# First-layer blocks 5 to 8 as two block pairs by seven products, instead of 7 and 8 alone

## The chip, the cores and the metric

One core of a Trainium2 chip. The metric is the device time of one execution in microseconds, as the median of several runs; the runs of the kernel before lie between 1590.37 and 1594.31 us. PE is TensorE (PEld its weight loads), DVE VectorE, ACT ScalarE, POOL GpSimd, SP SyncE, whose queue issues the DMAs.

## What is computed

Linear attention followed by two feed-forward layers, cut here to what matters:

```
kv  = einsum('bhsd,bhse->bhde', k, v)                 # B=8, H=8, S=576, D=64
o   = einsum('bhsd,bhde->bhse', q, kv)
x   = o / sqrt(mean(o*o, -1) + 1e-6) * g_norm         # then as 4608 tokens x 512
h   = x @ w_in1;   y   = (s * relu(h)**2 + b) @ w_out1    # 512 -> 2048 -> 512
h2  = y @ w_in2;   out = (h2 * sigmoid(h2)) @ w_out2      # 512 -> 2048 -> 512
```

The weights come as 8-byte floats and are turned into float32 by integer operations in the kernel. A product of float32 precision is made of three matmuls: every operand is split into a rounded part (hi) and a remainder (lo), and hi\*hi + hi\*lo + lo\*hi is accumulated.

## The kernel before

**Tiling.** The 4608 tokens are NB = 9 blocks of T = 512 tokens, features on the partitions. Block 8 collects the last 64 tokens of each of the 8 batches. A layer on one block alone ("plain") is 16 units of 128 hidden features (`unit`, L697 to L790): per unit 4 x 3 matmuls make h in a PSUM bank, ACT applies relu, square, scale and bias in place (L730, L733, L736) and rounds (L217), DVE makes the remainder `gh` (L220), and 4 x 3 matmuls add to the four output banks `acc`. That is 24 matmuls of 128 x 512 per unit, 384 per block.

**Pairs.** Two blocks go through a layer together by seven products instead of eight (Strassen-Winograd, a 2 x 2 product of token blocks by feature halves). The names are those of the code. Weights: eight factors A11, A12, A21, A22, S1 to S4 per set; a set covers one kind (in or out), one layer and two of the 16 weight tiles, so there are 32 sets (`factors`, L361 to L418). It recovers or decodes the four quarters, makes four sums (L393), rounds (L217) and makes remainders (L220), and stores all to DRAM in `w_d`. Tokens: B11, B21, B22 and T1 to T4, the last four from four subtractions (`pair_sums`, L846 to L873, over DRAM `xt_d`); `pair_x` loads them, rounds on ACT and makes the remainder on DVE or POOL.

Within a pair there are 8 steps j. `hidden(tp, j)` (L920 to L1028) does 7 x 2 x 3 matmuls into three PSUM banks X, Y, Z (line 936, `hp`), which hold sums of products; DVE adds them up (L961) into SBUF tiles `tmp`, ACT applies the function, differences T1 to T4 are made from `tmp` tiles on DVE or POOL (L1000), and each of seven g matrices is rounded on ACT (L217) and its remainder made on DVE or POOL (L220). `outputs(tp, q)` (L1049 to L1083) takes two steps j together: 14 groups of 6 matmuls, each into an `acc` bank which DVE adds to a running sum (L1073). `results` (L1085 on) adds up the seven sums on POOL (L1098) and stores them; for a first-layer pair it also makes the four token differences for the second layer in place (L1115). A pair is 8 x 42 + 4 x 84 = 672 matmuls.

**Order before.** First layer: blocks 0 to 6 plain, then blocks (7, 8) as a pair. Second layer: pairs (0,1), (2,3), (4,5), (7,8), then block 6 plain. NL1 (L174) is the number of first-layer pairs; `base(tp)` is the key at which pair tp begins, 112 + 32 tp.

**Beside the plain blocks** run: attention in 32 pairs of heads (`attention_pair`, eight batches by four), of which block t's are due during block t - 1; the decoding of the first layer's weights (`decode`); all 32 factor sets, spread evenly from key 19 to key 92; and the normalizing of block 8 (`last_block`). One unit is one key.

**What sets the order.** The program is written out by hand through `Plan` (L20 on): each operation has engines it may run on with a cost, a key, what it needs and makes, and the buffers that it takes and gives. `run` goes through them in simulated time, always takes the earliest that can begin (of those within 0.02 us the smallest key), and so fixes one order for every engine and for the SP queue. On the chip each engine works through its list in that order and waits by semaphores. A cost marked `Port` may not overlap another such cost in the plan; `both` lets DVE or POOL do it, `both2` also, without that mark.

**Buffers.** PSUM has eight banks: `acc` 4, `h` 2, `at` 2; in a pair X and Z come from `h`, Y from `at`. In SBUF 9 `tmp` tiles, 8 `rq` and 4 `rh` tiles of 128 x 256 for factors. Tiles of the first layer's resident weights are lent to the pairs when no plain block needs them any more (`lent_to`).

```
    NTMP = 9
    NRQ, NRH = 8, 4
...
    BANK = (X, Y, Z, X, Y, Y, Z)
...
        read = {3: "x1", 4: "u2", 5: "u3", 6: "h22"}
```

The last line says which product may only start when a DVE or ACT operation has read the bank that it adds to.

## Time and profile before

| what | value |
|---|---|
| runs shown, median of 3 | 1591.52 us |
| profiled execution: time / span of its instructions | 1591.99 / 1590.2 us |
| busy, of the span: PE, DVE, ACT, POOL | 99%, 67%, 57%, 44% |
| matmuls | 7500 |
| moved by DMA | 351 MB, 221 GB/s on average |

The span runs from the first to the last instruction of the program. A busy share is an average over stages of different kind. The PE figure counts a matmul from its start to its modelled end, and matmuls overlap, so the distance between starts tells what one costs. PEclk in the windows is the TensorE clock that was granted: 1.00 is 2.4 GHz, 0.50 is 1.2 GHz.

### The profile page before, as it was taken

The numbers are of one execution on the slowest core, as the hardware profiler recorded it, in microseconds if no ns is written. First come the engines' busy times: TensorE is split into PE (matmuls) and PEld (weight loads), VectorE is DVE, ScalarE is ACT, GpSimd is POOL, SyncE is SP. The second block draws the span as 40 slices with busy tenths as digits, with TensorE's granted clock in tenths as the row PEclk, the third lists the DMA queues.
The fourth block names the chain that finished last, engine by engine and source line by source line (L and its number), as shares of the span: only waits on it lengthen the run. The fifth ranks groups of instructions, "written<-read, shape, count | busy, mean of one in ns | idle before, by whom it ended". The sixth has DMA issues, their size and how long they took to land.

```text
span 1590.2 us, 23417 instructions
## 1 busy us (share of the span) xinstructions
PE 1572.8 (99%) x7500; PEld 1282.3 (81%) x7500; DVE 1068.8 (67%) x1811; ACT 898.5 (57%) x1720; POOL 693.5 (44%) x560
## 2 busy tenths in 40 slices
PE   8999999999999999999999999999999999999999
PEld 6877887878888888887888788888888888888887
DVE  5887677767767876535668966885688568856521
ACT  5997666666666777556767443545354445444222
POOL 1332121111122221123567886786678658865510
PEclk9999999999999999999999999999999999999999
DMA  8765767777677885896668786878687868876684
GB/s 214 196 190 155 249 209 239 225 207 220 197 202 226 247 235 169 287 350 213 189 194 260 230 271 194 284 200 236 188 295 194 238 194 261 199 240 188 210 210 134
DMA packets 377147, 351.31 MB, mean 221 GB/s; under 512 B 178240, under 2 KB 288832, under 8 KB 377024
## 3 DMA queue, kind: packets, MB, share of 16 engines
q1 hardware_dynamic: 376896, 349.81, 73.8%
q8 instruction: 60, 0.98, 0.3%
q14 instruction: 63, 0.52, 0.1%
q0 software_dynamic: 128, 0.00, 0.0%
HBM read 254.28 MB, written 95.42 MB: 220 GB/s over the span
## 4 chain that ended last, share of the span: by engine, by line
PE 88%; DMA 6%; DVE 2%; SPq 2%; ACT 2%; issue 1%; POOL 0%; DVEq 0%; ACTq 0%; POOLq 0%
PE hp L936 23%; PE acc L1064 8%; PE acc L1066 8%; PE acc L1065 8%; PE h L212 6%; PE h L213 6%; PE h L214 6%; PE acc L212 6%; PE acc L213 5%; PE acc L214 5%; SPq L229 2%; PE kv_ps L496 1%; PE acc L769 1%; PE acc L767 1%; PE acc L768 1%; DMA tmp<-y 1%
## 5 line engine op out<-in xcount | busy, mean ns | idle before, releaser
L936 PE MATMUL hp<-xo,win 128*128 128x512 f32 x1680 | 424.0, 390 | 2.9 <-DVE tmp L961 2.9
L936 PEld LDWEIGHTS hp<-xo,win 128*128 128x128 f32 x1680 | 315.1, 188 | 72.3 <-DVE tmp L961 4.6
L220 POOL TENSOR_TENSOR g<-tmp,g 128x512 fp32r<-128x512 f32 x168 | 238.2, 1426 | 223.6 <-ACT g L217 219.4
L1073 DVE TENSOR_TENSOR ya<-acc,ya 128x512 f32<-128x512 f32 x210 | 142.9, 685 | 116.7 <-PE acc L1066 116.2
L1064 PE MATMUL acc<-g,wout 128*128 128x512 f32 x560 | 219.6, 392 | 0.1
L1066 PE MATMUL acc<-g,wout 128*128 128x512 f32 x560 | 218.9, 391 | 0.0
L1065 PE MATMUL acc<-g,wout 128*128 128x512 f32 x560 | 218.9, 391 | 0.0
L217 ACT ACTIVATE g<-tmp 128x512 fp32r<-128x512 f32 x280 | 172.6, 629 | 78.4 <-POOL tmp L1000 31.2
L730 ACT ACTIVATE h<-h 128x512 f32<-128x512 f32 x128 | 74.6, 583 | 215.2 <-PE h L214 214.7
L212 PE MATMUL acc<-gh,wo 128*128 128x512 f32 x448 | 182.4, 407 | 0.7 <-DVE y L226 0.5
L212 PE MATMUL h<-xh,wi 128*128 128x512 f32 x448 | 176.9, 395 | 0.0
L213 PE MATMUL acc<-gh,wo 128*128 128x512 f32 x448 | 175.5, 392 | 1.2 <-DVE gh L220 1.2
L213 PE MATMUL h<-xl,wi 128*128 128x512 f32 x448 | 175.8, 392 | 0.2 <-DVE xl L220 0.2
L214 PE MATMUL h<-xh,wi 128*128 128x512 f32 x448 | 175.7, 392 | 0.0
L214 PE MATMUL acc<-gh,wo 128*128 128x512 f32 x448 | 175.0, 391 | 0.0
L961 DVE TENSOR_TENSOR tmp<-hp,tmp 128x512 f32<-128x512 f32 x200 | 136.6, 685 | 52.6 <-PE hp L936 49.2
L220 DVE TENSOR_TENSOR g<-tmp,g 128x512 fp32r<-128x512 f32 x112 | 150.7, 1365 | 18.3 <-ACT g L217 17.4
L322 POOL TENSOR_TENSOR rq<-raw 128x256 uint32<-128x256 uint32 x72 | 46.9, 652 | 253.3 <-DVE raw L308 133.5
L1000 POOL TENSOR_TENSOR tmp<-tmp 128x512 f32<-128x512 f32 x86 | 135.5, 1583 | 29.3 <-ACT tmp L982 15.5
L982 ACT ACTIVATE tmp<-tmp 128x512 f32<-128x512 f32 x120 | 75.5, 629 | 125.6 <-DVE tmp L961 125.2
L1066 PEld LDWEIGHTS acc<-g,wout 128*128 128x128 f32 x560 | 105.2, 188 | 23.4
L1064 PEld LDWEIGHTS acc<-g,wout 128*128 128x128 f32 x560 | 105.1, 188 | 23.3 <-DVE ya L1073 0.8
(137 smaller groups left out, 2682.0 us busy)
## 6 DMA issues: line engine op xcount, KB each, us to landing
wout<-wo SPq DMA_DIRECT2D x312, 256.0 KB, 3.7
win<-wi SPq DMA_DIRECT2D x120, 512.0 KB, 4.7
wi<-rq SPq DMA_DIRECT2D x192, 128.0 KB, 2.3
wo<-rq SPq DMA_DIRECT2D x192, 128.0 KB, 2.5
win<-wi SPq DMA_DIRECT2D x72, 256.0 KB, 3.7
raw<-in_moe_w_out_dram SPq DMA_DIRECT2D x38, 256.0 KB, 3.5
raw<-in_moe_w_in_dram SPq DMA_DIRECT2D x34, 256.0 KB, 3.5
xt_d<-tmp SPq DMA_DIRECT2D x32, 256.0 KB, 5.5
```

The costliest lines, as they stand in the source:

```text
L212: nc.tensor.matmul(ps, wh, xh, start=first, stop=False)
L213: nc.tensor.matmul(ps, wh, xl, start=False, stop=False)
L214: nc.tensor.matmul(ps, wl, xh, start=False, stop=last)
L217: nc.scalar.activation(hi, src, AF.Copy)
L220: eng[e].tensor_tensor(lo, src, f32(hi), op=ALU.subtract)
L936: nc.tensor.matmul(ps, w[:, wn, f_], x_[:, xn], start=first and n == 0, stop=kk == KH - 1 and n == 2, skip_group_check=True)
L961: nc.vector.tensor_tensor(t, bank[me, a], tmp[b_, me], op=ALU.add)
L1000: eng[e].tensor_tensor(t, tmp[a, me], tmp[b_, me], op=ALU.subtract)
L1064: nc.tensor.matmul(ps, w[:, 0, dd], gh, start=a == 0, stop=False)
L1065: nc.tensor.matmul(ps, w[:, 0, dd], gl, start=False, stop=False)
L1066: nc.tensor.matmul(ps, w[:, 1, dd], gh, start=False, stop=a == 1)
L1073: nc.vector.tensor_tensor(y2[tp, i, d], st["ps"], y2[tp, i, d], op=ALU.add)
```

## The change

Two first-layer pairs instead of one: blocks 0 to 4 run plain, then (5, 6) and (7, 8) as pairs; in the second layer (0,1), (2,3), (5,6), (7,8) are pairs and block 4 comes last, plain. Around it:

- The factor sets keep their order, but get keys by a broken line: the 16 first-layer sets from key 19 to 44, eight more to key 74, and the last eight together with four `pair_sums` of the second layer's pairs from 74 to 152, that is, during the two first-layer pairs (now keys 80 to 112 and 112 to 144). A set may not begin before the unit or hidden step of its key has started.
- A factor's hi and lo share one tile of 128 x 2 x 256, six of them, and are stored by one DMA. The second layer's `pair_sums` use these tiles too.
- The pool that holds them stays open until all sets are done (`turn3`); until then pairs do without two g tiles, three x tiles and one `tmp` tile.
- h21 and h12 stay in their PSUM banks Y and Z, the function is applied there, and the differences e, a2, f and c are all made on DVE with one operand in PSUM. Remainders from PSUM are on DVE; those of the other four g matrices, and all of `pair_x`, on POOL alone.
- Every PSUM bank is named by the plan; one `acc` bank passes to `h` when the pairs begin and back at their end.

```diff
-    NL1 = 1
+    NL1 = 2
...
-    NTMP = 9
-    NRQ, NRH = 8, 4
+    NTMP = 10
+    NRQ = 6
...
+    def started(key):
+        u = int(key)
+        if u < TP * KF:
+            return ("mm1o", u, 0)
+        n = (u - TP * KF) // 4
+        return ("hmo", n // NS, n % NS, 0, 0)
+
     def factors(layer, kind, j, key, before):
...
-        begin = [("full", n) + before for n in (S1, S2, S3, S4)] if before else [("w", 0, k_, m, 1) for k_, m in late]
+        begin = [started(key)] + (before or [("w", 0, k_, m, 1) for k_, m in late])
...
-            add({"SP": 0.48}, k2 + 0.03, lambda e, out_=out_: out_(e, 0), needs=[("fl", n) + me], makes=[("wd0", n) + me],
-                gives=[hb], move=0.36)
-            add({"SP": 0.48}, k2 + 0.04, lambda e, out_=out_: out_(e, 1), needs=[("wd0", n) + me], makes=[("wd", n) + me],
-                gives=[b[n]], move=0.36)
+            add({"SP": 0.48}, k2 + 0.03, lambda e, n=n: dma(w_d[layer, kind, j][:, n], w32[b[n]]), needs=[("fl", n) + me],
+                makes=[("wd", n) + me], gives=[b[n]], move=0.73)
...
+            if layer == 0 and t == TP - 1 and d == 0 and m == KF - 1:
+                plan.heir[acc] = "h"
...
-        add(both2(T), k2 + 0.02, lo, needs=[("pxh",) + me], makes=[("xo", i, tp, kk)], gives=[rb])
+        add({POOL: Port(1.3)}, k2 + 0.02, lo, needs=[("pxh",) + me], makes=[("xo", i, tp, kk)], gives=[rb])
...
+        in_bank = {"c": Y, "a2": Z, "a": Z}
...
-        add(both2(T), kt, minus("e", "a", "d"), needs=sg("a", "d"), makes=sg("e"), takes=[tb["e"]])
-        add(both2(T), kt + 0.02, minus("f", "b", "e"), needs=sg("b", "e"), makes=sg("f"), takes=[tb["f"]])
-        add(both2(T), kt + 0.01, minus("a", "b", "a"), needs=sg("b", "e"), makes=sg("a2"))
-        add(both2(T), kt + 0.1, minus("c", "c", "f"), needs=sg("f") + [("gl",) + me + (B21,)], makes=sg("c2"))
+        add({DVE: 0.69}, kt, add_up("e", B(Z), S("d"), ALU.subtract), needs=sg("a", "d"), makes=sg("e"), takes=[tb["e"]])
+        add({DVE: 0.69}, kt + 0.01, add_up("a2", S("b"), B(Z), ALU.subtract), needs=sg("b", "e"), makes=sg("a2"))
+        add({DVE: 0.69}, kt + 0.02, add_up("f", B(Z), S("d"), ALU.add), needs=sg("a2"), makes=sg("f"), takes=[tb["f"]])
+        add({DVE: 0.69}, kt + 0.1, add_up("c", B(Y), S("f"), ALU.subtract), needs=sg("f") + [("gl",) + me + (B21,)], makes=sg("c2"))
...
-            add(both2(T), kk + 0.03, lo, needs=[("gh",) + me + (i,)], makes=[("gl",) + me + (i,)],
+            add({DVE: 0.69} if src in in_bank else {POOL: Port(1.3)}, kk + 0.03, lo, needs=[("gh",) + me + (i,)],
+                makes=[("gl",) + me + (i,)], gives=gives)
...
-                add({POOL: 1.3}, key + 0.02 * n, go, needs=needs + ([o(0)] if n == 1 else []), makes=[o(n)], gives=[y(x) for x in gives])
+                add({POOL: Port(1.3)}, key + 0.02 * n, go, needs=needs + ([o(0)] if n == 1 else []), makes=[o(n)], gives=[y(x) for x in gives])
...
         sets = [(l, kind, j) for l in range(2) for j in range(NS) for kind in "io"]
+        for n, x in enumerate((26,28,30,32)):
+            sets.insert(x, (NL1 + n // KH, n % KH))
...
+        steps = ((0, KF + 3), (2 * NS, 44), (2 * NS + 8, base(0) - 6), (len(sets), base(NL1) + 8))
...
-            factors(*x, KF + 3 + (KF * (TP - 2) + 6 - KF) / len(sets) * n, sets[n - 1] if n else ())
+            after = token(sets[n - 1]) if n else []
+            if len(x) == 3:
+                factors(*x, set_key(n), after)
+            else:
+                pair_sums(*x, set_key(n), [started(set_key(n))] + after)
```

## Rows read from the trace of the kernel before

**Rows 1.** The page, part 1: span, busy time per engine (share of the span), instructions.

```profile
PE 1572.8 (99%) x7500; PEld 1282.3 (81%) x7500; DVE 1068.8 (67%) x1811; ACT 898.5 (57%) x1720; POOL 693.5 (44%) x560
```

**Rows 2.** The page, part 4: the chain that ended last, shares by engine.

```profile
PE 88%; DMA 6%; DVE 2%; SPq 2%; ACT 2%; issue 1%; POOL 0%; DVEq 0%; ACTq 0%; POOLq 0%
```

**Rows 3.** Windows: length, busy PE, PEld, DVE, ACT, POOL (instructions), PEclk, DMA share, GB/s.

```profile
50.00:140.00 90.00, 86.04 (x456) 69.60 (x455) 72.68 (x132) 79.20 (x162) 28.09 (x27) 0.97 0.69 181
340.00:440.00 100.00, 100.00 (x526) 81.51 (x525) 72.50 (x180) 66.75 (x146) 19.21 (x27) 1.00 0.73 212
640.00:735.00 95.00, 93.29 (x410) 76.23 (x408) 45.36 (x61) 51.93 (x87) 13.41 (x10) 1.00 0.92 310
735.00:889.00 154.00, 152.90 (x667) 124.97 (x668) 110.76 (x137) 108.73 (x182) 94.88 (x67) 1.00 0.68 216
1042.00:1195.00 153.00, 153.00 (x672) 125.83 (x671) 108.62 (x135) 69.78 (x118) 110.30 (x77) 1.00 0.78 231
135.00:145.00 10.00, 8.67 (x43) 6.60 (x44) 5.46 (x13) 6.23 (x15) 1.28 (x2) 0.66 0.81 191
```

**Rows 4.** Groups by line, whole span: count | busy us, mean ns | idle before, releaser.

```profile
L936 PE MATMUL hp<-xo,win 128*128 128x512 f32 x1680 | 424.0, 390 | 2.9 <-DVE tmp L961 2.9
```

**Rows 5.** Timeline of PE: start us, us, instruction; first product, then 49 matmuls.

```profile
724.93 0.85 PE L936 MATMUL hp<-xo,win 128*128 128x512 f32 x3
...
1479.34 0.39 PE L214 MATMUL h<-xo,win 128*128 128x512 f32 x1
...
1490.44 0.40 PE L1064 MATMUL acc<-g,wout 128*128 128x512 f32 x1
```

**Rows 6.** PE's waits, whole span: us in total, times, longest; the first.

```profile
PE hp L936 <- DVE tmp L961: 2.9, 4, 1.2
```

**Rows 7.** Timeline of PE near 136 us, idle before in brackets.

```profile
136.33 0.66 PE L523 MATMUL r_ps<-qT,kvf 128*128 128x64 f32 x2 [1.85 <-DVE qT L510]
...
137.75 0.63 PE L214 MATMUL h<-xh,wi 128*128 128x512 f32 x1
...
141.59 0.63 PE L214 MATMUL h<-xh,wi 128*128 128x512 f32 x1
```

**Rows 8.** Groups on DVE between 340 and 440 us, plain blocks.

```profile
L220 DVE TENSOR_TENSOR rq<-rq 128x256 fp32r<-128x256 f32 x35 | 14.2, 432 | 3.0 <-ACT rq L217 2.9
L220 DVE TENSOR_TENSOR gh<-h,gh 128x512 fp32r<-128x512 f32 x17 | 11.6, 682 | 2.9 <-ACT gh L217 2.8
L308 DVE SCALAR_TENSOR_TENSOR raw<-rq,raw 128x256 uint32<-128x256 uint32 x18 | 7.4, 413 | 0.3
...
L303 DVE TENSOR_SCALAR raw<-raw 128x256 uint32<-128x256 uint32 x18 | 5.6, 318 | 2.8 <-ACT rq L299 2.7
...
L598 DVE STREAM_TRANSPOSE sq<-rms 128x512 f32<-128x512 f32 x6 | 4.2, 708 | 0.1
...
L220 DVE TENSOR_TENSOR xl<-x,xh 128x512 fp32r<-128x512 f32 x4 | 2.7, 679 | 0.1
```

**Rows 9.** Groups of factors and pair sums, whole span.

```profile
L217 ACT ACTIVATE rq<-rq 128x256 fp32r<-128x256 f32 x192 | 75.3, 413 | 26.1 <-DVE rq L393 8.6 <-POOL rq L322 6.6 <-DMA wo<-rq 4.6
...
L322 POOL TENSOR_TENSOR rq<-raw 128x256 uint32<-128x256 uint32 x72 | 46.9, 652 | 253.3 <-DVE raw L308 133.5 <-DMA wi<-rq 24.5 <-ACT rq L217 16.0
...
L867 DVE TENSOR_TENSOR tmp<-tmp 128x512 f32<-128x512 f32 x32 | 25.9, 814 | 12.6 <-DMA tmp<-y 9.2 <-DMA tmp<-x_d 2.7
...
L393 POOL TENSOR_TENSOR rq<-rq 128x256 f32<-128x256 f32 x19 | 15.0, 789 | 59.1 <-DVE rq L393 22.2 <-DMA wi<-rq 16.8 <-DMA wo<-rq 13.1
```

**Rows 10.** Groups on DVE and POOL between 1042 and 1195 us, a second-layer pair.

```profile
L220 DVE TENSOR_TENSOR g<-tmp,g 128x512 fp32r<-128x512 f32 x22 | 29.9, 1381 | 4.2 <-ACT g L217 3.9
L1073 DVE TENSOR_TENSOR ya<-acc,ya 128x512 f32<-128x512 f32 x42 | 28.6, 684 | 23.4 <-PE acc L1066 23.3
L961 DVE TENSOR_TENSOR tmp<-hp,tmp 128x512 f32<-128x512 f32 x40 | 27.2, 683 | 10.0 <-PE hp L936 9.9
...
L220 POOL TENSOR_TENSOR g<-tmp,g 128x512 fp32r<-128x512 f32 x34 | 48.4, 1430 | 34.4 <-ACT g L217 33.6 <-POOL tmp L1000 0.7
```

More of the change, by code (lines that the diff above doesn't have):

```diff
@@ L951, in new @@
         def new(n):
-            t = tmp[n, me] = pools["l2p"].tile([P, T], F32, tag=f"tmp{plan.place[tb[n]]}", name="tmp")
+            t = tmp[n, me] = temp(tb[n])
             return t
@@ L968, in hidden @@
+        B = lambda n: lambda: bank[me, n]
+        S = lambda n: lambda: tmp[n, me]
         add({ACT: 0.59, DVE: 0.69}, k(0), x1, needs=done(0), makes=[("x1",) + me], takes=[tb["x1"]])
-        add({DVE: 0.69}, k(1), plus("a", Y, "x1"), needs=done(1) + [("x1",) + me], makes=[("u2",) + me], takes=[tb["a"]])
-        add({DVE: 0.69}, k(4), plus("b", Y, "x1"), needs=done(4) + [("u2",) + me], makes=[("u3",) + me], takes=[tb["b"]])
+        add({DVE: 0.69}, k(1), plus("u", Y, "x1"), needs=done(1) + [("x1",) + me], makes=[("u2",) + me], takes=[tb["u"]])
@@ L971, in hidden @@
+        add({DVE: 0.69}, k(4), plus("b", Y, "x1"), needs=done(4) + [("u2",) + me] + turn_, makes=[("u3",) + me], takes=[tb["b"]])
         add({DVE: 0.69}, k(4) + 0.05, plus("b", Z, "b"), needs=done(2) + [("u3",) + me], makes=[("h22",) + me])
-        add({DVE: 0.69}, k(5), plus("c", Y, "x1"), needs=done(5) + [("u3",) + me], makes=[("h21",) + me], takes=[tb["c"]],
-            gives=[tb["x1"], bk[Y]])
-        add({DVE: 0.69}, k(6), plus("a", Z, "a"), needs=done(6) + [("h22",) + me], makes=[("h12",) + me], gives=[bk[Z]])
@@ L976, in hidden @@
[L976 to L982 removed]
+        add({DVE: 0.69}, k(5), add_up("c", B(Y), S("x1"), ALU.add), needs=done(5) + [("u3",) + me], makes=[("h21",) + me],
+            gives=[tb["x1"]])
@@ new lines, in hidden, with curve @@
+        add({DVE: 0.69}, k(6), add_up("a", B(Z), S("u"), ALU.add), needs=done(6) + [("h22",) + me], makes=[("h12",) + me],
+            gives=[tb["u"]])
+        for src, ready, kk in (("d", done(3) + [("x1",) + me], k(3)), ("b", [("h22",) + me], k(4) + 0.1),
+                               ("c", [("h21",) + me], k(5) + 0.1), ("a", [("h12",) + me], k(6) + 0.1)):
+            def curve(e, src=src):
+                from_, to = (bank[me, X], new("d")) if src == "d" else (src_of(src), src_of(src))
+                nc.scalar.activation(to, from_, AF.Silu if layer_of(tp) else AF.Relu)
@@ L1157 @@
         make_identity(nc, ident)
-        kvf_t = [const.tile([P, P], F32, name=f"kvf{i}") for i in range(2)]
+        kvf_t = [ap.tile([P, P], F32, name=f"kvf{i}") for i in range(2)]
         lent["kvf"] = lend_flat("wi10", NP * P)
@@ L1211, with turn3 @@
         add({POOL: 0.0}, KF * (TP - 2) + 12, turn2,
-            needs=[("x1", t, p) for p in range(NP) for t in range(TP, NB)] + [("x32", NB - 1, p) for p in range(NP)]
-            + [("wd", n, l, kind, j) for n in range(8) for l in range(2) for kind in "io" for j in range(NS) if (n, l) != (A21, 0)],
-            makes=[("l2p",)])
+            needs=[("x1", t, p) for p in range(NP) for t in range(TP, NB)] + [("x32", NB - 1, p) for p in range(NP)], makes=[("l2p",)])
+        def turn3(e):
+            st_dec2.close()
+            pools["l2q"] = ctx.enter_context(tc.tile_pool(name="l2q", bufs=1, side="right"))
+        new = [(("g2", x), x) for x in ("l0", "l1")] + [(("xr", x), x) for x in ("r0", "r1", "r2")] + [(("tmp", "last"), NTMP - 1)]
+        for b_, x in new:
+            plan.settle(b_, x)
+        add({POOL: 0.0}, KF * (TP - 2) + 12, turn3,
+            needs=[("wd", n, l, kind, j) for n in range(8) for l in range(2) for kind in "io" for j in range(NS) if (n, l) != (A21, 0)]
+            + [("xs", o, *x) for o in SUMS for x in sets if len(x) == 2],
+            makes=[("l2q",)], gives=[b_ for b_, _ in new])
         add({POOL: 0.0}, -30, lambda e: None, makes=[("kvf0L",)])
```

150 lines of the change are left out of this document (78 added, 72 removed).

## The prediction

> **What bounds the kernel now.** I read the page's busy times first, then the chain that ended last, then the windows by stage, then PE's own waits. PE is busy 99% of the 1590.2 us span [rows 1], and 88% of the chain is PE work [rows 2]. The reader should see that no other engine reaches three quarters over the whole span; but the windows [rows 3] show stages. In the two windows of plain blocks, 50 to 140 and 340 to 440 us, DVE works 72 to 81%, ACT 67 to 88%, POOL 19 to 31%. While a block pair runs, POOL rises to 62 to 72%, DVE stays at 71 to 72%, and the DMA engines are at 0.68 to 0.78. So PE bounds every stage, and the price of a matmul is what a removed matmul gives back. The mean of 390 ns in [rows 4] is not that price: matmuls overlap. In [rows 5] 49 matmuls start in 1490.44 - 1479.34 = 11.10 us, 226.5 ns each.
>
> PE waits little: the longest kind is 2.9 us on the `tmp` sums [rows 6]. One stall matters as a pattern [rows 7]: PE stood 1.85 us before an attention matmul (`r_ps`, whose q came late), and then the granted clock fell: mean 0.66 from 135 to 145 us [rows 3], with matmuls 0.427 us apart (137.75 to 141.59, nine steps), which is 1.2 instead of 2.4 GHz. Some 12 matmuls paid 0.2 us more. A stall of 1.85 us cost about 1.85 + 2.4 = 4.3 us.
>
> **The change, part by part.**
>
> *Matmuls.* Two plain blocks are 2 x 16 x 24 = 768 matmuls, one pair is 8 x 7 x 6 + 4 x 14 x 6 = 672. The change turns two more plain blocks into a pair in the first layer; the second layer keeps three pairs from y1 plus one made in place, so it becomes two plus two, with one plain block at the end as before. 96 matmuls go: 96 x 0.2265 = **-21.7 us**, all on the path.
>
> *The plain stage becomes denser.* It shrinks from 112 units to 80, but still holds 32 attention pairs, all weight decoding and 24 to 25 of the 32 factor sets. The keys put twelve attention pairs of blocks 5 to 7 one per 2.67 units between units 16 and 46, beside the usual four per block, so 0.625 pairs per unit there, and sixteen first-layer sets between units 19 and 44, 0.64 per unit. In the window 340 to 440 there are 17 `gh` remainders [rows 8], so a unit takes 5.88 us: 24 x 0.2265 = 5.44 us, and the rest, 0.44 us x 17 = 7.5 us, belongs to about five attention pairs, 1.5 us each. A dense unit then needs 5.44 + 0.625 x 1.5 = 6.4 us of PE. DVE needs per unit 0.68 (`gh`), 0.25 (x remainder and y copies), 0.625 x 4.4 = 2.75 for attention (five operations of about 0.7 us, of which one row stands in [rows 8], and small ones) and 0.64 x 12 x 0.42 = 3.2 for sets: 6.9 us, more than PE. What relieves it is that a set's sums and remainders may go to POOL (0.79 us each, [rows 9]), which is at 19%; with two per unit moved DVE is at 6.1 of 6.4 us. The nearest stretch as dense is 50 to 140 us, where DVE was at 81% and ACT at 88% [rows 3], and the one stall of [rows 7] ended it: one per 90 us. The dense stretch is 29 x 6.4 = 186 us, so two stalls by that count; but there ACT was the fuller engine, and ACT, 67% between 340 and 440, gains only a third of an attention pair per unit here; I take one: **+4.3 us**. Ends: 0 and five stalls, +21 us.
>
> *Pairs: DVE reads PSUM.* The sums of h, three differences and three remainders now work from PSUM. Such operations took 683 and 684 ns beside a busy POOL, while the remainders of g, read from SBUF alone, took 1381 ns there [rows 10], and such a remainder (`xl`) 679 ns while POOL was at 19% [rows 8]. DVE gets 12 such operations per j, 96 x 0.684 = 65.7 us per pair, and 42 x 0.684 = 28.7 us of output sums, some 5.5 us of copies: 100 us, where it had 109 to 111 [rows 3]. POOL gets 32 remainders of g, 14 of x and, late, 14 to 22 result sums. In the second layer this leaves both engines freer than before: 0 us; it is hidden under PE's 672 x 0.2265 = 152.2 us per pair.
>
> *The first-layer pairs carry sets.* Three sets and two pair sums of the second layer fall into each. A set is 4 x (0.32 + 0.41 + 0.32) for decoding, 4 x 0.41 for sums and 8 x 0.43 for remainders, 9.3 us of DVE [rows 8] (the third decoding operation taken like the first, a sum like the second); pair sums are 8 x 0.81 = 6.5 us [rows 9]. DVE has 100 + 28 + 6.5 = 134 us. No row shows these 80 small operations beside a busy POOL. Below they add nothing; above each waits as the SBUF remainders do, 1381 - 679 = 0.70 us [rows 8, 10]: +56 us. I take the price between, 0.70 us times POOL's busy share, since an operation that finds POOL idle should run as in [rows 8]. In the second pair POOL has (32 + 14 + 22) x 1.43 + 12 x 0.65 = 105 of 152 us [rows 9, 10], 69%: 80 x 0.48 = +39 us, 173 us. If half of the 36 sums and remainders move to POOL, 18 x 0.91 = 16 us go: 157 against 152. In the first pair there are no results to add up yet and outputs start a quarter late; the same working gives about 140 us, under PE. So **+5 us**, ends 0 and, with nothing moved and every wait full, 38 + 30 = +68 us. ACT goes from 109 us [rows 3] to at most 109 + 3 x 12 x 0.413 [rows 9] = 124 us: covered.
>
> By the Trainium skill, SBUF — State Buffer, section "SBUF: two separate sides", the port pair that DVE and GpSimd share is an exclusive lock, held for a whole instruction, against DVE operations with two SBUF inputs; by it every set operation that meets POOL would wait as long as the remainders of g, and the sum would be that of B below. The trace agrees as far as 1381 against 679 ns goes; set operations beside a busy POOL are in no row.
>
> *Banks, buffers, queues.* Output sums get three banks instead of four; a group of six matmuls is 1.36 us and its sum 0.684 us, and DVE idles 23.3 us before those sums waiting for PE [rows 10]: 0 us while DVE keeps up. Six rounding tiles of double width replace eight and four: each factor goes out in one DMA rather than two, fewer issues on SP: 0 us. Fewer g and x buffers until the sets are done: outputs free two g tiles in every four groups of six matmuls, 5.4 us, and need T1 only six steps in: 0 us, covered by that distance.
>
> *DMA.* The pair stage moved 216 GB/s. Three sets (twelve transfers of 256 KB each, 3.15 MB), two pair sums (2 x 2.1 MB) and the previous pair's results (4.2 MB) add 62 + 28 + 28: 334 GB/s in the second pair. The most any shown window moved is 310, at a DMA share of 0.92 [rows 3]. If 310 were the ceiling, that pair would take 334/310 x 152 = 164 us, +12; 216/0.68 = 318 suggests less. I take 0, because loads are issued several products ahead and only one pair is over: ends 0 and +12.
>
> **Sum**, against the profiled execution's 1592.0 us (span 1590.2 and 1.8 around it): 1592.0 - 21.7 + 4.3 + 5 = 1579.6. The median of the runs shown, 1591.5, lies 0.5 lower: **1579 us**, 0.8% faster.
>
> **Rivals.**
>
> *A, the weights come late.* SP issues in order; a factor store waiting for its remainder stands before the next loads, and the second pair wants more than the stage ever moved. Then the 12 us come on top: 1579 + 12 = **1591**, no change. For it: 0.92 at 310 GB/s [rows 3]. Against: the largest of PE's waits [rows 6] is on DVE, and of the 14 kinds in that view none is on the load of a weight.
>
> *B, DVE bounds the first-layer pairs.* The full 0.70 us on all 80 operations, half of the sums and remainders moved: 134 + 56 - 18 x 1.13 = 170 us in the second pair, some 162 in the first: 18 + 10 = 28 us, plus 4.3: 1591.5 - 21.7 + 32.3 = **1602**, slower. It decides once the two pairs together lose over 22 us, DVE above about 163 us in each. For it: [rows 10]. Against: many waits fall where POOL stands idle for ACT.
>
> *C, the sets are not done in time.* The next pair reads factors some 20 keys (95 us) after the last set is due; only a long lag would turn this into a wait. About 30 us late: 1609.
>
> **Chances.** A measurement here can tell 0.3% (4.8 us) from no change. Forecast and its neighbourhood (0 to two stalls, DVE 0 to 7 us over): 0.65. A: 0.14. B: 0.18, C: 0.03. Faster 0.65, same 0.14, slower 0.21. The range starts where nothing stalls and the 2.9 us of [rows 6] go too, 1591.5 - 21.7 - 2.9 = 1567, and ends at 1603, which takes in B's own value.
>
> **What would show it.** The first product should start near 725 - 2 x 16 x 5.44 = 551 us rather than at 725 [rows 5]. Each pair should take 152 to 158 us; the first two, most of all the second, longer than the rest. In them set remainders on DVE should take up to 1.1 us instead of 0.43, and PE's waits should name `tmp` sums. I am wrong if a first-layer pair takes over 165 us, if PE's waits name weight loads, or if the plain units between 16 and 46 hold over 9 us of waits with the granted clock falling more than twice.

## The result, and the profile after

The changed kernel takes 1611.4 us (median of four runs, 1609.05 to 1612.71) beside 1591.73 us for the kernel before in the same session: ratio 1.0112, 95% interval 1.0099 to 1.0125. It is **slower by 1.1%**. The forecast was 1579 us, 0.8% faster, and the result lies above the end of the range, 1603. The profiled execution took 1612.7 us with a span of 1610.9, so it is 1.3 us over the median.

Busy times of the page of the kernel after, against [rows 1]:

```profile
PE 1567.3 (97%) x7404; PEld 1266.9 (79%) x7404; DVE 1091.3 (68%) x1928; ACT 913.2 (57%) x1782; POOL 644.5 (40%) x591
```

The 96 matmuls are gone, as the forecast counted. By the price of [rows 5] that is worth 21.7 us, so a kernel that loses no more than the one before would have a span of 1590.2 - 21.7 = 1568.5 us. The span is 1610.9: **42.4 us were lost elsewhere**. PE's timeline of the kernel after shows where (start, us, engine, line; the first product, products with which four of the later pairs begin, and the last):

```profile
558.35 0.85 PE L947 MATMUL hp<-xo,win 128*128 128x512 f32 x3
...
705.71 1.75 PE L947 MATMUL hp<-xo,win 128*128 128x512 f32 x7
...
868.77 2.21 PE L947 MATMUL hp<-xo,win 128*128 128x512 f32 x9
...
1033.21 1.52 PE L947 MATMUL hp<-xo,win 128*128 128x512 f32 x6
...
1187.37 1.52 PE L947 MATMUL hp<-xo,win 128*128 128x512 f32 x6
...
1497.59 0.84 PE L947 MATMUL hp<-xo,win 128*128 128x512 f32 x3
```

Pairs overlap by a few matmuls, so I count 336 `hp` matmuls to a pair; the starts are then 558.4, 706.6, 869.9, 1033.9, 1188.0 and 1343.4 us, and the products of the last pair end at 1498.0. Before, they were 722.2, 863.8, 1017.9, 1171.3 and 1324.8, with the end at 1478.0. (The 724.93 that [rows 5] calls the first product is not the first: that list begins at 725 us. So the start that the prediction works out as 551 us is 548.)

| stretch | before | after | lost |
|---|---|---|---|
| plain stage | 722.2, less 32 units x 5.44 = 548.1 | 558.4 | 10.3 |
| first pair (first layer) | 141.6 | 148.2 | 6.6 |
| second pair (first layer) | 153.5, mean of a later pair | 163.3 | 9.8 |
| third pair (second layer, blocks 0 and 1) | 153.5 | 164.0 | 10.5 |
| three further pairs | 153.5 each | 154.1, 155.4, 154.6 | 3.6 |
| the end | 112.2 | 112.9 | 0.7 |

These come to 41.5 us; the other microsecond is that a later pair took 153.5 us before, not the 152.2 of 672 matmuls at 226.5 ns: inside a pair they stood 228.3 ns apart. The windows of the kernel after, with the columns of [rows 3]:

```profile
458.00:558.00 100.00, 92.48 (x403) 74.88 (x402) 61.56 (x118) 64.82 (x128) 29.56 (x30) 1.00 0.86 292
558.00:706.00 148.00, 141.47 (x604) 113.48 (x603) 115.79 (x209) 105.88 (x201) 68.01 (x68) 0.99 0.85 278
706.00:870.00 164.00, 159.68 (x683) 129.67 (x682) 135.97 (x224) 110.32 (x204) 104.58 (x92) 0.98 0.93 306
870.00:1034.00 164.00, 157.03 (x668) 125.38 (x667) 112.67 (x174) 79.14 (x143) 98.81 (x80) 0.99 0.83 268
1034.00:1188.00 154.00, 154.00 (x673) 126.05 (x672) 98.09 (x152) 69.63 (x119) 76.18 (x60) 1.00 0.77 229
...
573.00:578.00 5.00, 5.00 (x16) 3.95 (x16) 4.27 (x7) 3.65 (x8) 2.15 (x3) 0.66 0.99 360
778.00:786.00 8.00, 6.91 (x18) 5.43 (x19) 4.76 (x7) 5.06 (x10) 4.74 (x5) 0.57 1.05 374
949.00:953.00 4.00, 4.00 (x13) 3.05 (x12) 2.03 (x3) 1.55 (x3) 4.00 (x4) 0.57 1.03 388
```

No compute engine but PE is full in any of the five stages: in the second pair DVE is busy 136 of 164 us, 83%. Yet PE stands idle in every stage up to 1034 us, and the granted clock falls three times in the pairs, as the last three lines show. In these three short windows the share of the DMA engines is 0.99, 1.05 and 1.03, so they are full there (second pair: 0.93). Nothing like this was there before, where PE was busy 152.9 us of 154 in a pair [rows 3].

PE's waits of the kernel after, against [rows 6] (what PE waited with, for what; us in total, times, longest):

```profile
PE hp L947 <- DVE tmp L972: 10.2, 9, 2.5
PE acc L211 <- DVE gh L218: 7.5, 4, 3.5
PE acc L1080 <- DVE ya L224: 2.9, 1, 2.9
...
PE acc L1080 <- ACT ya L222: 1.9, 1, 1.9
PE hp L947 <- DMA win<-wi: 1.5, 2, 1.0
```

Between 558 and 1034 us PE's idle times come to 17.8 us in 18 places: `tmp` 10.2, result tiles `ya` 2.9 + 1.9, all others 2.9. The half-clock stretches there last 3.4, 6.8 and 3.4 us, and half of that, 6.8 us, is lost. Together 24.6, of the 26.9 us that the first three pairs lost; matmuls that stand 1.1 ns further apart (last section) make 2 more.

**What a `tmp` wait is.** Products 4, 5 and 6 may add to bank Y or Z only when DVE has read it (the sums of L972, once L961: u2, u3, h22). The tightest is u3: it reads Y after product 4, and product 5 waits for it, in seven of the nine `tmp` waits; the other two (588.07 and 829.98) are product 6 for h22. DVE does its list in order. Its timeline in the kernel after, at two of the waits:

```profile
826.23 0.69 DVE L1089 TENSOR_TENSOR ya<-acc,ya 128x512 f32<-128x512 f32 x1
828.57 0.30 DVE L320 TENSOR_SCALAR raw<-raw 128x256 uint32<-128x256 uint32 x1 [1.65 <-DMA raw<-in_moe_w_out_dram]
829.04 0.29 DVE L305 TENSOR_SCALAR raw<-raw 128x256 uint32<-128x256 uint32 x1 [0.17 <-ACT rq L301]
829.25 0.68 DVE L972 TENSOR_TENSOR tmp<-hp,tmp 128x512 f32<-128x512 f32 x1
...
923.77 4.16 DVE L218 TENSOR_TENSOR rq<-rq 128x256 fp32r<-128x256 f32 x3
927.85 0.68 DVE L972 TENSOR_TENSOR tmp<-hp,tmp 128x512 f32<-128x512 f32 x1
```

PE's timeline at the same places, and POOL's at the second:

```profile
829.98 0.50 PE L947 MATMUL hp<-xo,win 128*128 128x512 f32 x1 [1.11 <-DVE tmp L972]
...
928.58 0.73 PE L947 MATMUL hp<-xo,win 128*128 128x512 f32 x2 [1.16 <-DVE tmp L972]
...
924.74 5.57 POOL L1114 TENSOR_TENSOR ya<-ya 128x512 f32<-128x512 f32 x4
```

In the first, the decoding of a set stood in front of the sum and waited 1.65 us for its own load; DVE was idle meanwhile, and PE then stood 1.11 us. In the second, three remainders of a set, 0.43 us each in [rows 8], took 4.16 us beside POOL. A set operation has no hurry, but the sum behind it has.

This does not hold for all nine. In five of them (572.79, 588.07, 607.10, 829.98 and 928.58; 7.4 us of the 10.2) set operations stand in DVE's list shortly ahead of the sum; at 572.79 and 607.10 the set operation had itself waited 0.65 and 1.48 us for a buffer that one of the sets' stores had to free. In one (0.3 us) it is a pair sum. In the other three (2.5 us) there is no such work: at 585.01 and 944.80 DVE stood ready and PE waited out the sum's own 0.69 us, and at 886.21 output sums and differences filled the list.

### The profile page after: what moved, and what is told of

Same layout as the page of the kernel before. It is cut to its first block, busy times and chain, and to the rows that moved or that the text cites. A ratio compares the mean times of both kernels' runs of the same rounds, so it can differ in the third digit from the quotient of the medians.

```text
span 1610.9 us, 23435 instructions
## 1 busy us (share of the span) xinstructions
PE 1567.3 (97%) x7404; PEld 1266.9 (79%) x7404; DVE 1091.3 (68%) x1928; ACT 913.2 (57%) x1782; POOL 644.5 (40%) x591
## 4 chain that ended last, share of the span: by engine, by line
PE 51%; DMA 4%; DVE 3%; POOL 1%; issue 1%; SPq 1%; ACT 0%; DVEq 0%; POOLq 0%; ACTq 0%
PE hp L947 22%; PE acc L1080 8%; PE acc L1082 8%; PE acc L1081 8%; DMA raw<-in_moe_w_out_dram 1%; PE acc L772 1%; PE acc L771 1%; PE acc L770 1%; PE h L212 1%; PE h L210 1%; PE h L211 1%; SPq L227 1%; DMA raw<-in_moe_w_in_dram 1%; DMA win<-wi 1%; DMA wout<-wo 1%
## 5 line engine op out<-in xcount | busy, mean ns | idle before, releaser
L947 PE MATMUL hp<-xo,win 128*128 128x512 f32 x2016 | 517.7, 394 | 13.7 <-DVE tmp L972 10.2
L947 PEld LDWEIGHTS hp<-xo,win 128*128 128x128 f32 x2016 | 379.3, 189 | 104.8 <-DVE tmp L972 14.4
L1080 PE MATMUL acc<-g,wout 128*128 128x512 f32 x672 | 265.6, 395 | 4.7 <-DVE ya L224 2.9
L1081 PE MATMUL acc<-g,wout 128*128 128x512 f32 x672 | 264.6, 394 | 0.9 <-POOL g L218 0.9
L1082 PE MATMUL acc<-g,wout 128*128 128x512 f32 x672 | 264.1, 393 | 0.0
L1080 PEld LDWEIGHTS acc<-g,wout 128*128 128x128 f32 x672 | 126.7, 189 | 33.2 <-DVE ya L224 3.3
L1081 PEld LDWEIGHTS acc<-g,wout 128*128 128x128 f32 x672 | 126.8, 189 | 29.3 <-POOL g L218 1.8
L1082 PEld LDWEIGHTS acc<-g,wout 128*128 128x128 f32 x672 | 126.9, 189 | 29.0
L215 ACT ACTIVATE g<-tmp 128x512 fp32r<-128x512 f32 x192 | 120.9, 629 | 33.4 <-DVE tmp L986 22.5
L211 PE MATMUL acc<-gh,wo 128*128 128x512 f32 x320 | 125.9, 393 | 7.5 <-DVE gh L218 7.5
L210 PE MATMUL acc<-gh,wo 128*128 128x512 f32 x320 | 131.7, 411 | 0.0
L210 PE MATMUL h<-xh,wi 128*128 128x512 f32 x320 | 127.6, 399 | 0.2 <-ACT xh L215 0.2
L212 PE MATMUL h<-xh,wi 128*128 128x512 f32 x320 | 125.8, 393 | 0.0
L212 PE MATMUL acc<-gh,wo 128*128 128x512 f32 x320 | 125.3, 392 | 0.0
L215 ACT ACTIVATE g<-hp 128x512 fp32r<-128x512 f32 x144 | 85.8, 596 | 61.1 <-DVE tmp L986 25.5
L986 DVE TENSOR_TENSOR hp<-hp,tmp 128x512 f32<-128x512 f32 x144 | 99.5, 693 | 29.0 <-PE hp L947 28.5
L1114 POOL TENSOR_TENSOR ya<-ya 128x512 f32<-128x512 f32 x84 | 108.6, 1320 | 26.2 <-DVE ya L1089 21.8
```

What stands on the lines that cost most here:

```text
L210: nc.tensor.matmul(ps, wh, xh, start=first, stop=False)
L211: nc.tensor.matmul(ps, wh, xl, start=False, stop=False)
L212: nc.tensor.matmul(ps, wl, xh, start=False, stop=last)
L215: nc.scalar.activation(hi, src, AF.Copy)
L947: nc.tensor.matmul(to, w[:, wn, f_], x_[:, xn], start=first and n == 0, stop=kk == KH - 1 and n == 2, skip_group_check=True)
L986: nc.vector.tensor_tensor(t, a(), b_(), op=op)
```

## The experiments

**The question.** Theory: the sets that run during the pairs stand in DVE's list in front of what PE waits for. Rivals: their transfers crowd out the weights (A); the edits to banks and PSUM cost by themselves; three `acc` banks are too few. After the first batch a further one: the fixed order of the plan, which changes with every edit.

**1. The edits without the pair, and the pair without the edits.** The first kernel takes NL1 back to 1; all other edits stay, and sets and pair sums lie evenly over the plain stage. The second sets NL1 = 2 in the kernel before, nothing else.

```diff
-    NL1 = 2
+    NL1 = 1
...
-        for n, x in enumerate((26,28,30,32)):
+        for n, x in enumerate((26,28,30,32,34,36)):
...
-        steps = ((0, KF + 3), (2 * NS, 44), (2 * NS + 8, base(0) - 6), (len(sets), base(NL1) + 8))
+        steps = ((0, KF + 3), (len(sets), base(0) - 14))
```

> The changed kernel with one first-layer pair again (blocks 7 and 8), all factor sets spread evenly up to key 98 before it, as in the kernel before; what stays of the change is h in PSUM banks, differences on DVE, remainders on POOL, three banks for the output sums, one DMA per factor. The matmuls are those of the kernel before. If these edits cost nothing by themselves, 1591 us give or take 3; if three output banks or POOL-only remainders are what costs in the changed kernel, each pair loses 2 to 5 us and it is 1600 or more.

> The kernel before with two first-layer pairs and nothing else: 96 matmuls less, all 32 factor sets between keys 19 and 57, that is within blocks 1 to 3. If the denser plain stage is what costs, it loses more there than the changed kernel's 10 us (20 to 60), and its pairs run at 154 us each: 1600 to 1630. If only the sets beside the pairs cost, this kernel is near 1570 to 1580.

Measured: 1612.6 us, ratio 1.0130 (1.0106 to 1.0153), for the first (e1), and 1719.7 us, 1.0798 (1.0773 to 1.0823), for the second (e2). The first seemed to put the whole loss on the edits. But it did not place the sets as the kernel before does: pair sums stood between sets, the last remainder of a set ran at 798 us (623 before), and PE stood 2.3 and 3.8 us for DVE at 753 and 763 us, in the first pair. So it was made again with the sets' keys up to 92, as before, and the pair sums after them:

```diff
-        for n, x in enumerate((26,28,30,32)):
-            sets.insert(x, (NL1 + n // KH, n % KH))
+        sets += [(NL1 + n // KH, n % KH) for n in range(6)]
...
-        steps = ((0, KF + 3), (2 * NS, 44), (2 * NS + 8, base(0) - 6), (len(sets), base(NL1) + 8))
+        steps = ((0, KF + 3), (4 * NS, base(0) - 20), (len(sets), base(0) - 8))
```

> A cleaner form of the run with one first-layer pair: the PSUM, POOL, buffer and DMA edits of the change, one first-layer pair, all 32 sets between keys 19 and 92 as in the kernel before, the six pair sums of the second layer after them (keys 92 to 104). In the first such run the pair sums stood between the sets and waited for blocks not yet computed. If the edits are free without a second pair: 1591 to 1595. If they cost by themselves, as the first run's 1613 says: 1605 or more.

Measured (e12): 1603.6 us, 1.0070 (1.0052 to 1.0088). **The edits without the second pair cost about 11 us**: the first pair starts at 726.5 instead of 722.2, and its pairs take 143.2, 154.1, 154.5, 154.5 and 155.4. Not all of this is shown to be the price of banks and PSUM, for the keys are as before but the times are not: a set now waits for the unit of its key, the last remainder of a set runs at 733 us, and 46 of the 61 recorded subtractions for pair sums run inside the first pair (before: 3 of 63). The second kernel's 8% are no price of the pair either. Its sets last until 625 us, 47 of the 64 subtractions for pair sums run after the first pair has begun, and PE stands 50.5 us for the first pair's x (592 to 643 us) and 35.8 us in one piece inside that pair, which takes 191 us; its later pairs, at 153 to 155, are as before.

**2. The last eight sets.** The first kernel leaves them out (the second layer's pairs then read the sets of j - 4). The second works on them and leaves out only their stores. The third leaves out the work on them and keeps their loads and stores.

```diff
...
+                if x[0] and x[2] >= NS // 2:
+                    continue
                 factors(*x, set_key(n), after)
...
```

> The changed kernel without the last eight factor sets (second layer, j = 4 to 7): nothing loads, decodes, sums or stores them, and the second layer reads the sets of j - 4 in their place; the four pair sums stay where they are. If the sets beside the pairs are what costs, the first three pairs return from 148, 163 and 164 us to about 142, 154 and 154: some 27 us less, 1584. If the hand-over of the result tiles and banks between pairs costs, the stalls at 779 and 948 us stay and it is 1600 or more.

> The changed kernel where the last eight sets are loaded, decoded, summed and rounded, but not stored; the second layer reads the sets of j - 4. 16.8 MB of writes less. Leaving these sets out altogether gave 1589, keeping them 1611. If it is their work on DVE beside POOL that holds PE up, this stays at 1605 or more; if it is DMA load (0.93 of the engines in the second pair), most of the 22 us goes: below 1597.

> The counterpart: of the last eight sets only the transfers stay, four loads and eight stores of 256 KB each, the stores straight from the loaded tiles; no engine works on them; the second layer reads the sets of j - 4. If DMA load is the cause: 1600 to 1611. If the engines' work is the cause: 1589 to 1595.

Measured: 1588.9 us, 0.9966 (0.9955 to 0.9978), without the sets (e3); 1606.3, 1.0078 (1.0061 to 1.0095), without their stores (e5); 1597.7 (ten runs, 1591.7 to 1603.6), 1.0029 (1.0013 to 1.0045), with transfers alone (e6). The windows of the kernel without the last eight sets, its first three pairs, and its wait on `tmp`:

```profile
555.00:697.00 142.00, 139.04 (x606) 113.22 (x605) 91.20 (x139) 94.93 (x162) 51.27 (x40) 1.00 0.70 219
697.00:853.00 156.00, 154.51 (x672) 125.42 (x671) 103.86 (x161) 104.53 (x178) 88.35 (x69) 1.00 0.83 270
853.00:1008.00 155.00, 155.00 (x677) 126.80 (x676) 94.09 (x145) 72.30 (x126) 87.95 (x71) 1.00 0.77 242
...
PE hp L950 <- DVE tmp L975: 3.0, 3, 1.3
```

Without them these pairs take 141.7, 156.5 and 154.3 us, and the clock stays up. So the last eight sets are worth 1.0112 - 0.9966 = 1.46%, **23 us**. The traces account for it: PE's idle time in the three pairs goes from 17.8 to 4.4 us, the 6.8 us of half clock go, and the first product starts 3.2 us earlier. Both waits for result tiles at 779 and 948 us go as well, so they too hang on the sets, or on the order that the sets give. Without the stores 18 us remain, with transfers alone 10. These overlap and don't add up, but the work on the engines is the larger part and the transfers the smaller, so rival A is there in part, though not where A looked for it: PE's waits for weights are 1.5 us. DVE, not PE, waits for loads, those of the sets themselves: between 706 and 1034 us of the kernel after 5.4 us in five places, the longest 2.3.

**3. Where the sets' sums and remainders run.** Of the last eight sets, on POOL alone, and on DVE alone (shown: the remainders on POOL).

```diff
...
-            add(both(QW), k2 + 0.02, lo, needs=[("fh", n) + me] + [x for r in readers[n] for x in full(r)], makes=[("fl", n) + me])
+            add({POOL: both(QW)[POOL]} if layer and j >= NS // 2 else both(QW), k2 + 0.02, lo, needs=[("fh", n) + me] + [x for r in readers[n] for x in full(r)], makes=[("fl", n) + me])
```

> The changed kernel with the sums and remainders of the last eight sets on POOL alone (12 of a set's 24 two-engine operations). If the number of operations in front of DVE's work for PE is what counts, 3 to 8 us less than 1611; if it is the time for which the SBUF operations of the two engines exclude one another, POOL's 0.74 us in place of DVE's 0.42 makes it worse: 1612 to 1625.

> The counterpart: those sums and remainders on DVE alone. In the second pair 16 of 23 remainders and 6 of 11 sums are there already, so little moves: 1608 to 1616. More than 8 us worse would say that DVE's queue is the whole cost; better than 1606 would say that excluded time is.

Measured: 1602.5 us (nine runs, 1597.8 to 1607.1), 1.0057 (1.0041 to 1.0073), on POOL (e13), and 1617.9, 1.0161 (1.0130 to 1.0191), on DVE (e14). PE's waits on `tmp`, the kernel with POOL alone:

```profile
PE hp L947 <- DVE tmp L972: 7.7, 8, 1.6
```

and with DVE alone:

```profile
PE hp L947 <- DVE tmp L972: 14.2, 10, 3.3
PE acc L211 <- DVE gh L218: 7.4, 4, 3.5
PE acc L1080 <- DVE ya L224: 3.9, 2, 3.2
PE acc L1080 <- ACT ya L222: 3.1, 1, 3.1
```

POOL alone, either, DVE alone: the wait goes 7.7, 10.2, 14.2 us and the time 1602.5, 1611.4, 1617.9. (The profiled execution is the second fastest of nine for the first, 3 us under the median, and for the last the slowest, 7 to 9 us above the other three, so the waits differ more than the medians.) On POOL such an operation takes 739 to 754 ns, on DVE alone 784 to 831, about the same; what differs is whether it stands in the list that PE waits on. The direction fits the theory, but the two steps, 9 and 6.5 us, are no larger than what the order alone moves (part 6), and the second is under the 8 us that the expectation asked for.

**4. Banks and remainders.** No `acc` bank handed to `h` (four banks for output sums; X and Z then take turns in two); then the remainders of x and of g from SBUF on DVE or POOL, as before the change.

```diff
-            if layer == 0 and t == TP - 1 and d == 0 and m == KF - 1:
-                plan.heir[acc] = "h"
...
-        if me == (NPP - 1, NS - 1):
-            plan.heir[bk[Z]] = "acc"
```

```diff
...
-            add({DVE: 0.69} if src in in_bank else {POOL: Port(1.3)}, kk + 0.03, lo, needs=[("gh",) + me + (i,)],
+            add({DVE: 0.69} if src in in_bank else both2(T), kk + 0.03, lo, needs=[("gh",) + me + (i,)],
```

> The changed kernel with no bank handed over: four banks for output sums and two for X and Z during the pairs. If PE waits for output sums because there are three banks, the stalls at 779 and 948 us (2.9 and 1.9 us, with their half clock some 9 us) go: 1602. If two banks for X and Z hold up the products, every one of 48 steps j may lose up to a us: 1611 to 1640.

> The changed kernel with the remainders of x and of the g matrices read from SBUF again allowed on DVE or POOL, as before the change. If POOL alone is too slow for them (PE waited 1.2 us for xo and 0.9 us for g on POOL), 2 to 5 us less: 1607. If DVE is the engine in front of PE, more work on it costs: 1615 to 1630.

Measured: 1634.3 us, 1.0264 (1.0244 to 1.0284), with four banks (e4), and 1648.8, 1.0353 (1.0338 to 1.0369), with the remainders on either engine (e7). With four banks PE waits 14.1 us for remainders of g out of a bank, the longest 8.8. With the remainders on either engine, which puts more work into DVE's list, it waits 18.2 us on `tmp` and 16.2 for output sums. Both edits of the change earn their place in this kernel, as far as one order each can tell: the bank 24 us, the remainders on POOL 38 us.

**5. The plan's costs.** The plan counts 0.7 us before a transfer's own time and 1.1 after it, 2.5 us in all for 256 KB, where such transfers took 3.3 to 5.4 us from issue to landing (medians by kind, page of the kernel after, part 6). And it counts 0.34 us for a 256-wide operation on DVE, where [rows 8] has 0.43. The first kernel raises both, the second only the landing; the third puts both into the kernel before.

```diff
-    DMA_START, DMA_END = 0.7, 1.1
+    DMA_START, DMA_END = 0.7, 2.5
...
-        return {DVE: Port(0.07 + n * 1.05e-3), POOL: Port(0.15 + n * 2.36e-3)}
+        return {DVE: Port(0.15 + n * 1.05e-3), POOL: Port(0.2 + n * 2.2e-3)}
```

> The changed kernel, same work, with two costs of the plan nearer to the trace: a transfer lands 2.5 us after its bytes instead of 1.1, and a 256-wide operation between SBUF tiles takes 0.42 us on DVE instead of 0.34. Only the order on the engines and queues changes. If PE is held up because DVE stands in its fixed order before a load or store that lands later than planned, other work gets in front and 8 to 15 us go: 1596 to 1603. If load itself (DVE or DMA) is the cause, it stays within 3 us of 1611.

> Of the two plan costs (together 1604) the landing time alone. If what helped is that DVE no longer stands before loads and stores that land late, this keeps most of the 8 us: 1602 to 1606. If it was the true length of set operations, 1608 to 1613. If small changes of order move the time by as much anyway, it may fall outside both.

> The kernel before with the two plan costs of the run that reached 1604 (landing 2.5 us, 0.42 us for a 256-wide DVE operation). A control: PE stands for only 13 us in its trace, so there is little to win, 1585 to 1592. If these costs are worth 8 us whatever the kernel, it comes out near 1584.

Measured: 1603.6 us, 1.0068 (1.0053 to 1.0083), with both (e8); 1609.1, 1.0104 (1.0078 to 1.0131), with the landing (e15); 1665.3, 1.0459 (1.0443 to 1.0476), in the kernel before (e11). In the changed kernel both costs gain 7 us and the landing alone nothing that the intervals tell; in the kernel before both lose 73, where at most a gain was expected: its first pair starts at 732.5 and takes 200 us, and PE stands 31.8 us in one piece before 803.6. The costs don't make the order better as such; they make another order.

**6. Further remedies.** On the kernel with both costs: one more tile for results (a 15th `ya`, one `tmp` less), and the additions of results on DVE or POOL. Then the sets stretched eight keys further (with both costs), POOL alone for the late sets with both costs, and POOL alone for the late sets and for the second layer's pair sums.

```diff
-        steps = ((0, KF + 3), (2 * NS, 44), (2 * NS + 8, base(0) - 6), (len(sets), base(NL1) + 8))
+        steps = ((0, KF + 3), (2 * NS, 44), (2 * NS + 8, base(0) - 6), (len(sets), base(NL1) + 16))
```

> The changed kernel with the two plan costs (1604) and one tmp tile turned into a fifteenth tile for output sums. PE waited 8.0 us there for copies of output sums, which wait for a result tile whose store has not landed. If the tiles run short by one or two at the hand-over of a first-layer pair, 3 to 8 us less: 1596 to 1600. If it is the POOL chain of 22 additions that is late, one tile gives 0 to 2 us.

> The changed kernel with the two plan costs (1604), and the additions of results allowed on DVE (0.69 us) as well as POOL (1.3 us). If the POOL chain holds the result tiles, 3 to 8 us less: 1596 to 1600. If DVE in front of PE is the tighter place, as the run with remainders on both engines says (1649), 0 to 15 us more.

> The two plan costs and the last sets spread to key 160 rather than 152: one set or pair sum per 7.2 keys instead of 6.5, the last ones in the third pair, where ACT and DVE have room. If the density in the first-layer pairs costs in proportion, 10% of some 14 us: 1600 to 1603; if the shorter supply of g, x and tmp tiles in the third pair costs more, 1605 or more.

> Both edits that helped: the last eight sets' sums and remainders on POOL alone (1602.5) and the two plan costs (1603.6). If the two losses are separate (DVE's queue in the pairs; the order at the end of the plain stage), they add up: 1592 to 1598, level with the kernel before. If both only shuffle the order, 1600 to 1610.

> The run at 1602.5 with the second layer's sixteen token differences in these pairs on POOL alone as well. If every operation taken off DVE's queue helps, 1 to 4 us less, 1598 to 1601; if POOL, which PE already waits for (2.3 us for xo), is now as tight, 1603 to 1610.

Measured, in this order: e9 1607.9 us, 1.0099 (1.0080 to 1.0118); e10 1619.1, 1.0172 (1.0154 to 1.0190); e16 1611.4, 1.0108 (1.0084 to 1.0131); e17 1611.6, 1.0118 (1.0099 to 1.0136); e18 1613.1, 1.0126 (1.0106 to 1.0146). None gains on the kernel that it starts from (e8 for the first four, e13 for the last), although each expectation names a gain for one of its cases. Most telling is the fourth: POOL alone gave 9 us and the costs 7, both together give nothing; its third pair alone takes 170 us. So a difference of some 10 us between two such kernels can be the order's, not the edit's. No kernel that does the whole work beat the one before.

## Why the prediction was wrong

**Right.** The matmuls: 96 fewer; with the last eight sets left out (e3) the kernel is faster than the one before, for all that the edits cost. (At the 228.3 ns of a pair the term is 20.5 us, not 21.7.) The demand: POOL 104.6 us in the second pair where 105 was worked out, in part by luck, since its operations were shorter (1.32 to 1.39 us, not 1.43) and twelve set operations were added; the transfers 306 GB/s over 164 us, which over 152 is 330 where 334 was worked out, and a share of 0.93. Where PE would wait: on `tmp` sums in the first-layer pairs, and not on weights; only the longest pair was the third, not the second. A set remainder beside POOL: 788 ns in the mean of the second pair, between the 432 of [rows 8] and the bound of 1.1 us; single ones took up to 1.5. The DVE groups of the second pair in the kernel after:

```profile
L218 DVE TENSOR_TENSOR g<-hp,g 128x512 fp32r<-128x512 f32 x24 | 16.5, 687 | 7.3 <-ACT g L215 6.7 <-issue 0.3
L972 DVE TENSOR_TENSOR tmp<-hp,tmp 128x512 f32<-128x512 f32 x24 | 16.4, 682 | 0.8 <-PE hp L947 0.7
L218 DVE TENSOR_TENSOR rq<-rq 128x256 fp32r<-128x256 f32 x16 | 11.9, 788 | 0.6 <-ACT rq L215 0.5
...
L873 DVE TENSOR_TENSOR rq<-rq 128x512 f32<-128x512 f32 x8 | 8.2, 1027 | 1.0 <-DMA rq<-y 0.9
L224 DVE COPY ya<-acc 128x512 f32<-128x512 f32 x10 | 6.8, 685 | 3.4 <-PE acc L1082 1.8 <-DMA xt_d<-ya 1.5
...
L403 DVE TENSOR_TENSOR rq<-rq 128x256 f32<-128x256 f32 x6 | 4.2, 704 | 0.2
```

Operations with one operand in PSUM keep their 682 to 687 ns beside POOL, as forecast. The pure SBUF ones are longer, a remainder by 0.36 us, half of the full 0.70. By the Trainium skill, SBUF — State Buffer, section "SBUF: two separate sides", a DVE operation with two SBUF inputs and a GpSimd operation take an exclusive lock: whichever starts first has it for its whole instruction, and the other is blocked. The trace agrees for single ones (three in 4.16 us at 923.77, in the third pair). In the second pair POOL was busy only 64%, and the mean shows it. The prediction took from the rule that every set operation waits, although 24 of its 80 operations have one input; beside POOL those took longer too (last section).

**The step that failed: the first-layer pairs carry sets, +5 us.** It set DVE's sum (157 us; measured, 136) against PE's 152 and called the rest covered. Measured, the last eight sets cost 23 us (after against e3), although DVE was 83% busy. The forecast asked whether DVE has the time, not what stands in front of u3 in its list. A set operation delays u3 by its own wait for a load, a buffer or POOL, and u3 has little to spare: only output groups that lie between products 4 and 5 cover it. The trace shows it in five of the nine `tmp` waits. E13 and e14 move the work without removing it and point the same way, but by themselves they prove nothing, since their steps are no larger than those of the order. The other part of the 23 us, the two waits for result tiles and their half clock, goes with the sets too, by which link is not shown. The rule that the queues of VectorE, ScalarE and GpSimd are strictly first in, first out is in the Trainium skill, PSUM — Partial Sum Buffer, section "Engine vs sequencer instructions", and the two DVE rows at 828.57 and 923.77 agree with it. Two prices were left out besides: the third pair, which still has the last of the sets and the second pair's results (+10.5 us, forecast 0), and the clock, which fell beside three of the stalls (6.8 us, forecast only for the plain stage).

**Banks, hand-over: forecast 0.** Two of the larger stalls are here. PE's timeline of the kernel after:

```profile
779.09 0.80 PE L1080 MATMUL acc<-g,wout 128*128 128x512 f32 x1 [2.87 <-DVE ya L224]
...
948.31 0.50 PE L1080 MATMUL acc<-g,wout 128*128 128x512 f32 x1 [1.85 <-ACT ya L222]
```

DVE's, ahead of the first of them:

```profile
778.34 0.69 DVE L224 COPY ya<-acc 128x512 f32<-128x512 f32 x1 [0.57 <-DMA xt_d<-ya]
```

and POOL's:

```profile
766.13 8.31 POOL L1131 TENSOR_TENSOR ya<-ya 128x512 f32<-128x512 f32 x6
774.40 0.74 POOL L403 TENSOR_TENSOR rq<-rq 128x256 f32<-128x256 f32 x1
775.10 1.29 POOL L1131 TENSOR_TENSOR ya<-ya 128x512 f32<-128x512 f32 x1
```

The next pair's first sum must leave its `acc` bank for a result tile, which is free only when POOL's additions of the pair before are done and stored. The distance was measured to DVE's idle time [rows 10], where four banks stood; the chain over POOL and the stores was not followed. In the kernel with both costs (e8) PE waits 8.4 us for such copies, with one tile more (e9) 2.7 and with DVE's help (e10) 0.3. So both edits take these waits away, and yet both kernels are slower than e8: PE's wait on `tmp` is 3.9 us in e8, 9.7 in e9 and 14.7 in e10. What the hand-over alone is worth stays open.

**PSUM edits: forecast 0, "leaves both engines freer".** They do (98 and 76 us against 109 and 110 in [rows 3]), but PE gains nothing by it, and the kernel with the edits and one first-layer pair takes 11 us more (e12). Of that, 4.3 us were lost before the first pair and 1.6 in it, where that kernel runs pair sums; in the pairs the matmuls are 1.2 ns further apart, which makes 4.0 us over five pairs.

**The plain stage: +4.3 forecast, 10.3 lost**, in the range given (0 to 21), but not where it was looked for: in the dense units 16 to 46 (144 to 352 us) PE stood only 2.6 us. It waited for remainders `gh` four times between 470 and 515 us, units 65 to 72, 7.5 us in all. DVE and POOL of the kernel after, before the longest (3.52 us, ended at 514.02); DVE:

```profile
504.63 3.44 DVE L873 TENSOR_TENSOR tmp<-tmp 128x512 f32<-128x512 f32 x2
...
509.87 1.49 DVE L218 TENSOR_TENSOR rq<-rq 128x256 fp32r<-128x256 f32 x1
511.28 1.75 DVE L873 TENSOR_TENSOR tmp<-tmp 128x512 f32<-128x512 f32 x1
512.95 0.41 DVE L218 TENSOR_TENSOR rq<-rq 128x256 fp32r<-128x256 f32 x1
513.29 0.68 DVE L218 TENSOR_TENSOR gh<-h,gh 128x512 fp32r<-128x512 f32 x1
```

POOL:

```profile
509.46 3.03 POOL L218 TENSOR_TENSOR xo<-x,xo 128x512 fp32r<-128x512 f32 x2 [1.94 <-ACT xo L215]
```

The first pair's x remainders, now on POOL alone, its pair sums and set operations fall together there, ahead of `gh`. That is the same fault, a busy share instead of a place in the list.

**The sum, by what was measured**: 1592 - 21.7 (matmuls) + 11 (e12) + 23 (last eight sets) = 1604. Up to 1.0112 x 1592 = 1610 some 5 us remain, and the denser plain stage fits them: e3 starts its first product at 555.2 instead of 548, 7 us, of which up to 4.3 may already be in the 11. How much of the 11 and the 23 is owed to the particular order, and would go with a better one, stays open: the remedies moved the time by as much and did not add up.

**Rivals and signs.** B had the side right and nearly the mechanism, but priced it by DVE's load, 170 us, which never came, so that its 1602 lies nearer than the forecast is in part luck. C's 1609 lies nearest, and that is luck altogether: PE waits for no factor in the third pair, and its 1.5 us of waits for weights are in the last two pairs. None of the three signs set up for "wrong" was clearly reached (163.3 us for a first-layer pair against 165; 1.5 us of waits for weights; 2.6 us of waits in the units 16 to 46 against 9). The first three pairs lost 27 us without any of them. The 0.21 for slower was too little: pair, banks and PSUM edits were set near 0 by the same argument, that an engine has time to spare.

## What to carry to other kernels

Work that fills idle time of an engine is only free if it cannot stand in front of what the critical engine waits for: ask of each filler what its own wait is (a load, a buffer, another engine) and who is queued behind it, not whether the engine has time left. Where a fixed order is generated, any edit, also to a cost, gives another order worth some 10 us here, and once 73 (e11). A variant that leaves a part out (e3) or moves it (e13, e14) has a new order too, so its time is read together with the waits in its trace. Where several terms are set to 0 for the same reason, they can fail together.
